# Attention, an ELU MLP and a soft mixture of experts in one kernel: row maxima in one pass of PE, combine weights after the slot inputs, more and longer expert loads

## The chip, the core and the metric

The kernel runs on one core of a Trainium2 chip. The metric is the device time of one execution in microseconds, the median of three runs; the profile is one further execution. TensorE is PE in the profile, VectorE DVE, ScalarE ACT, GpSimd POOL, SyncE SP.

## What is computed

The output of an attention (4 batches, 8 heads, 1152 keys, 576 pooled queries, 64 wide) goes through an ELU MLP and then a soft mixture of experts, all in fp32. Cut to its core:

```python
q_pool = q.reshape(B, H, S // 2, 2, D).mean(axis=3)
scores = scale * np.matmul(q_pool, k.transpose(0, 1, 3, 2))
scores = scores - np.max(scores, axis=-1, keepdims=True)
attn = np.exp(scores); attn = attn / (attn.sum(-1, keepdims=True) + 1e-09)
x = (attn @ v) as [2304 tokens, 512]
h = x @ w_in                                  # [512, 2048]
x = np.where(h > 0, h, np.exp(np.minimum(h, 0)) - 1) @ w_out
logits = x @ phi                              # 8 experts x 4 slots = 32 columns
d = softmax of logits over the tokens; slot_input = d.T @ x
slot_out[e] = np.maximum(slot_input[e] @ w1[e], 0) @ w2[e]   # w1[e] [512, 1024], w2[e] [1024, 512]
c = softmax of logits over the slots; out = c @ slot_out
```

## The kernel before

**Order of the work.** Every operation is handed to a planner (class Plan, line 51) with `add(t, engines, durations, fn, r, w)`: a due time t, the engines that may do it, an estimated duration on each, what it reads and writes. `run` simulates the five queues and sets each engine's instructions in a fixed order; where an operation may go to ACT, DVE or POOL, the cost in `BIAS` of its phase (0 attention, 1 MLP, 2 experts, 3 preparation) is added before the earliest end wins, and `PRI` shifts due times by class. On the chip each engine works through its queue in that order and waits on semaphores. The due times come from constants such as `SLOT`, `OFF`, `TM2`, `EAV`.

**Attention.** 16 pairs of heads. `prep_q` and `prep_k` transpose q and k of a pair and split them into a rounded part and a rest. `max_unit` and the carried part of `step` compute scores for the row maxima alone (line 596), `max_red` reduces them on DVE into MX (line 605). `max_end` (line 633) finishes them: DVE reduces to one column of MZ, PE multiplies MZ by the identity (`row`, line 642) so that the maxima of half the queries (288) lie in a row of a PSUM bank psC, and ACT writes the negated row to nm (line 649). `step` then computes transposed scores, 128 keys by 288 queries by two heads, as four fp32r products, the last of which adds nm (line 664); ACT takes the exponential (676), PE multiplies with v in fp32 into psC (671), and POOL or DVE sums the exponentials (685).

**MLP.** 32 slots: eight groups of 256 hidden columns times four batches (batches 0 to 2 first, then batch 3). In each slot `h_mm` (line 828) multiplies with w_in, `elu` makes the activation on ACT and DVE (839, 840, 842) and splits it into a rounded part (cast, line 500) and a rest (subtraction, line 503), and `o_mm` (line 867) multiplies with w_out into psC, which DVE adds to X (line 878). `split_w` and `split_x` split weights and inputs in the same way; subtractions may go to DVE or POOL. The first stretch also holds `decode` (lines 457 to 497), which prepares the weights: seven DVE steps, of which the addition (line 477) may go to POOL.

**Soft mixture.** `logits` or `logits_split`, then `col_max` (softmax over tokens) and `tok_all` per batch: transposes of X (1030), slot inputs (1034), and in the same function the combine weights: row maximum, exponential (1047), splitting (1001 to 1003), transposes (1053) into C3T.

**Experts.** The expert weights are 64 loads of 512 KB (units), issued by SP (line 1176). `spare` declares the slots of 4 KB per partition that come free as memory of earlier stages dies: 18 of them before the MLP ends, seven in the region z when it has ended; later units reuse slots. `stage1` (1191) multiplies the slot inputs with w1, four experts side by side in 32 columns each; `stage2` (1219) multiplies with w2, first the output columns 0 to 255 (m=0) of all experts into one bank, then columns 256 to 511 (m=1). `finish` (1232, 1250) turns each half into output tiles, scaled by ACT or DVE, and stores them in three pieces.

Of the kernel before, what the change touches and what calls it, by code (L numbers as in the profile page):

```python
# [50 lines left out]
class Plan:  # L51
# [11 lines left out]
    def add(self, t, eng, dur, fn, r=(), w=(), size=0.0, mode="F", port=False, fixed=False):  # L63
# [218 lines left out]
def attention_moe_softmoe(  # L282
# [112 lines left out]
    r0 = zr + 2 * KD * NQ  # L395
# [10 lines left out]
    MZ = carve("f", "MZ", 1, 2 * len(NT5) * D)[0].rearrange("p (a j m) -> p a j m", j=2, m=D)  # L406
# [41 lines left out]
    DN = carve("f", "DN", 1, len(NT5) * NS)[0]  # L448
# [59 lines left out]
    nc.vector.memset(r32(MEM["v"][:, :512]), 1.0)  # L508
    nc.vector.memset(MZ, 0.0)
# [816 lines left out]
```

## Time and profile before

| what | value |
|---|---|
| three runs | 1018.55, 1019.13 (median), 1020.74 us |
| profiled execution | 1019.5 us, its span 1017.7 us |
| PE busy | 979.6 us, 96% |
| DVE, POOL, ACT busy | 690.6, 591.7, 498.4 us |
| HBM read, written | 100.27 MB, 13.18 MB |

The span runs from the first to the last instruction. Busy time is time in which an engine has an instruction in work; a PE that is busy may still be slowed by its operands. The attention stage lasts to some 470 us, the MLP from there to 921, the expert stage to the end. Records of neighbours on one engine can overlap, since an instruction starts before the one ahead of it has fully ended.

### The profile page before, as it was taken

To read this page: it belongs to the slowest core of one execution; us is meant where nothing else is said; L and a number is where in the kernel's file an instruction comes from. 1 tells how busy PE (TensorE), PEld (TensorE's weight loads), DVE (VectorE), ACT (ScalarE), POOL (GpSimd) and SP (SyncE) were. 2 spreads that over 40 slices of the span, in tenths; PEclk is the share of its full clock that TensorE was granted. 3 is DMA by queue.
4 is the path that set the end of the run, shared out by engine and by line. 5 is a ranking of instruction groups with operands and counts; after the bars stand their busy time and mean duration, and the time that the engine had idled before them with its cause. 6 is when DMAs were issued, how large, how long until landed. Compare 5 with 4: busy or idle time off the path is not lost.

```text
span 1017.7 us, 21700 instructions
## 1 busy us (share of the span) xinstructions
PE 979.6 (96%) x8838; PEld 806.5 (79%) x8838; DVE 690.6 (68%) x1141; ACT 498.4 (49%) x886; POOL 591.7 (58%) x389
## 2 busy tenths in 40 slices
PE   7999999999999999999999999999999999998884
PEld 6777777767777777777799999999999999995332
DVE  4776687899888777779888788776446565654000
ACT  1455555656555555556665344444335665533022
POOL 1679889877989889887754544444227345330000
PEclk9899999999999999999999999999999999999856
DMA  7233324234334431212344333535031123124998
GB/s 168 48 84 71 96 68 117 62 106 114 83 84 105 110 80 45 65 36 85 105 142 139 116 103 115 166 119 180 24 104 41 62 85 105 62 84 148 342 348 299
DMA packets 111827, 114.92 MB, mean 113 GB/s; under 512 B 43632, under 2 KB 83056, under 8 KB 111728
## 3 DMA queue, kind: packets, MB, share of 16 engines
q1 hardware_dynamic: 111728, 113.55, 37.7%
q8 instruction: 69, 1.13, 0.5%
q14 instruction: 30, 0.25, 0.1%
HBM read 100.27 MB, written 13.18 MB: 111 GB/s over the span
## 4 chain that ended last, share of the span: by engine, by line
PE 84%; DVE 8%; DMA 3%; ACT 2%; issue 1%; SPq 0%; ACTq 0%; POOL 0%; DVEq 0%; POOLq 0%
PE psA L828 20%; PE psC L867 19%; PE psC L671 13%; PE psA L664 9%; PE psS L664 5%; PE psA L596 3%; DVE memf L605 2%; DMA memf<-in_moe_w_dram 2%; PE psS L596 2%; PE psA L1191 2%; PE psC L695 1%; PE psC L642 1%; PE psC L705 1%; ACT memf L676 1%; DVE memf L544 1%
## 5 line engine op out<-in xcount | busy, mean ns | idle before, releaser
L685 POOL TENSOR_TENSOR memf<-memf 128x576 f32<-128x576 f32 x246 | 369.7, 1504 | 60.8 <-ACT memf L676 37.4
L867 PE MATMUL psC<-memr,memz 128*128 128x288 f32 x1512 | 225.3, 297 | 2.4 <-ACT memf L500 2.3
L867 PEld LDWEIGHTS psC<-memr,memz 128*128 128x128 f32 x1512 | 207.9, 189 | 6.0 <-ACT memf L500 3.4
L605 DVE TENSOR_REDUCE memf<-psA 128x2 f32<-128x384 f32 (+3 forms) x248 | 161.7, 665 | 50.1 <-ACT memf L676 32.9
L671 PE MATMUL psC<-memf 128*64 128x288 f32 x1152 | 171.3, 419 | 0.0
L503 POOL TENSOR_TENSOR memr<-memf,memr 128x576 fp32r<-128x576 f32 x57 | 87.4, 1537 | 139.8 <-ACT memr L500 120.7
L878 DVE TENSOR_TENSOR memf<-psC,memf 128x288 f32<-128x288 f32 x220 | 99.3, 459 | 96.1 <-PE psC L867 94.8
L676 ACT ACTIVATE memf<-psA 128x576 f32<-128x576 f32 x190 | 122.9, 651 | 78.5 <-PE psA L596 61.2
L828 PE MATMUL psA<-memr,memz 128*128 128x288 f32 x768 | 140.7, 296 | 0.0
L828 PEld LDWEIGHTS psA<-memr,memz 128*128 128x128 f32 x768 | 114.9, 188 | 0.2
L671 PEld LDWEIGHTS psC<-memf 128*64 128x64 f32 x1152 | 69.9, 136 | 48.6 <-issue 8.9
L605 DVE TENSOR_REDUCE memf<-psS 128x2 f32<-128x384 f32 (+3 forms) x127 | 84.0, 661 | 27.2 <-ACT memf L676 17.8
L839 ACT ACTIVATE memf<-psA 128x576 f32<-128x576 f32 x64 | 41.7, 651 | 121.5 <-PE psA L828 120.5
L503 POOL TENSOR_TENSOR memz<-memf,memz 128x1024 fp32r<-128x1024 f32 x23 | 56.4, 2452 | 49.9 <-ACT memz L500 49.9
L676 ACT ACTIVATE memf<-psS 128x576 f32<-128x576 f32 x98 | 63.8, 651 | 35.4 <-PE psS L596 30.1
L500 ACT CAST memr<-memf 128x576 fp32r<-128x576 f32 x87 | 57.3, 673 | 45.2 <-DVE memf L842 40.6
L828 PE MATMUL psA<-memr,memv 128*128 128x288 f32 x384 | 78.2, 296 | 0.0
L664 PE MATMUL psA<-memr 64*128 64x288 f32 x744 | 66.3, 300 | 0.6 <-ACT memf L676 0.3
L828 PEld LDWEIGHTS psA<-memr,memv 128*128 128x128 f32 x384 | 61.7, 188 | 0.8 <-issue 0.4
L664 PEld LDWEIGHTS psA<-memr 64*128 64x128 f32 x744 | 54.4, 185 | 8.3 <-issue 4.4
L664 PE MATMUL psA<-memy 64*128 64x288 f32 x582 | 58.2, 305 | 0.0
L842 DVE SCALAR_TENSOR_TENSOR memf<-memf,psA 128x576 f32<-128x576 f32 x64 | 47.8, 746 | 10.7 <-ACT memf L840 10.7
(206 smaller groups left out, 1542.0 us busy)
## 6 DMA issues: line engine op xcount, KB each, us to landing
memf<-in_moe_w_dram SPq DMA_DIRECT2D x38, 512.0 KB
memf<-wscr SPq DMA_DIRECT2D x32, 512.0 KB
memz<-in_q_dram SPq DMA_DIRECT2D x32, 288.0 KB
memz<-in_k_dram SPq DMA_DIRECT2D x32, 288.0 KB
memf<-in_v_dram SPq DMA_DIRECT2D x16, 576.0 KB
memf<-in_moe_w_in_dram SPq DMA_DIRECT2D x32, 256.0 KB
wscr<-memf SPq DMA_DIRECT2D x32, 256.0 KB
memf<-in_moe_w_out_dram SPq DMA_DIRECT2D x16, 512.0 KB
```

Source lines behind the costliest of these rows:

```text
L500: return lambda e: nc.scalar.copy(out_, in_) if e == "ACT" else nc.vector.tensor_copy(out_, in_)
L503: return lambda e: ENG[e].tensor_tensor(out_, a, b, ALU.subtract)
L596: nc.tensor.matmul(tile_[:m, j, lo : lo + n * MW], lhsT=qkb["qh", i][js, o : o + m], rhs=qkb["kh", i][js, g * MW : (g + n) * MW], start=Tr ...
L605: add(t, "DVE", dve(2 * n * MW), lambda: nc.vector.reduce_max(MX[i][:m, a, :, g : g + n], v4(got(psS, tok)[:m, :, lo : lo + n * MW], n), a ...
L664: nc.tensor.matmul(sp[:, j, :NH], lhsT=qkb[w, i][js, cs] if w else ONER[js], rhs=qkb[m, i][js, hs], start=(x == 0), stop=(x == 3))
L671: nc.tensor.matmul(psC[h][j * D : (j + 1) * D, :NH], lhsT=VR[i][:, j, c], rhs=e[:, j], start=(c == 0), stop=(c == NC - 1))
L676: add(t + 0.01, "ACT", act(NQ, True), lambda: nc.scalar.activation(got(EAf, E_), got(psS, S_)[:, :, :NH], AF.Exp, scale=1.0 / 16.0), r=[S_ ...
L685: ENG[e].tensor_tensor(ac, a, got(EAf, E_), ALU.add)
L828: nc.tensor.matmul(ph[:, t, :NH], lhsT=a, rhs=x, start=(i == 0), stop=(i == 3 * KD - 1))
L842: add(t + 1.2, "DVE", dve(NQ), lambda: nc.vector.scalar_tensor_tensor(got(Ef, uk), got(Uf, ek), -1.0, ph(), ALU.add, ALU.max), r=[ek, A], ...
L867: nc.tensor.matmul(po_(), lhsT=a, rhs=x, start=(i == 0), stop=(i == 3 * GF - 1))
L878: add(t0 + 0.8, "DVE", dve(NH), lambda: nc.vector.tensor_tensor(d, po_(), d, ALU.add), r=[ck], w=XK)
```

## The change

Parts, in the order of the program:
- `max_end`: MZ and the identity (IDR) are fp32r, MZ holds 32 columns per head instead of 64, so both heads make one product of 64 output rows: three matmuls instead of six. ACT writes two pieces of 32 rows, and nm is cleared once at the start.
- `max_red` of a carried part is ordered behind the exponential of the same bank.
- The split inputs x of batches 1 and 3 move from region r to region z, which grows by 4.5 slots.
- `tok_all` keeps the slot inputs; the combine weights become `combine(b, t)`, due after the slot inputs of all batches, with a copy of the logits (DN) for each batch.
- Region z gives eleven late slots instead of seven. Units: w1 per expert with whole rows (4 KB runs), w2 of experts 0 to 5 with whole rows (2 KB runs), w2 of the last two experts by halves as before (1 KB runs). `stage2` does both halves of an expert together, but for the last two.
- Output stores are due behind the last load ("loads").
- The planner's numbers are new: `PRI` has 80 entries, `BIAS`, `LOOK`, `SLOT`, `OFF`, `TM2` and others change, and loads of phase 2 count for 0.75 of their size.

```diff
-BIAS = [{'DVE': 2.612, 'Pool': 1.8312, 'ACT': 1.5924}, {'DVE': 3.8592, 'Pool': 2.61, 'ACT': -4.78}, {'DVE': 7.9625, 'Pool': 27.723, 'ACT': 7.0754}, {'ACT': -9.5594, 'Pool': -3.8076, 'DVE': -9.6637}]
+BIAS = [{'DVE': 2.6845, 'Pool': 1.8955, 'ACT': -0.4027}, {'DVE': -3.2955, 'Pool': 5.8552, 'ACT': -4.78}, {'DVE': 7.9625, 'Pool': 25.9664, 'ACT': 7.8882}, {'ACT': -14.3311, 'Pool': 2.7731, 'DVE': -2.1432}]
...
-    MZ = carve("f", "MZ", 1, 2 * len(NT5) * D)[0].rearrange("p (a j m) -> p a j m", j=2, m=D)
+    MZ = carve("v", "MZ", 1, len(NT5) * D)[0].rearrange("p (a j m) -> p a j m", j=2, m=D // 2)
+    IDR = carve("v", "IDR", 1, P)[0]
...
+    for i in range(2):
+        nc.gpsimd.memset(r32(qkb["nm", i]), 0.0)
...
-                for j in range(2):
-                    nc.tensor.matmul(psC[h][j * D : (j + 1) * D, lo - h * NH : hi - h * NH], lhsT=MZ[:, a, j], rhs=ident[:, lo - o : hi - o],
-                                     start=True, stop=True)
+                nc.tensor.matmul(psC[h][:D, lo - h * NH : hi - h * NH], lhsT=MZ[:, a].rearrange("p j m -> p (j m)"), rhs=IDR[:, lo - o : hi - o],
+                                 start=True, stop=True)
...
-        add(t, "PE", 0.476, row, r=[("MZ", 0, a) for a in tiles], w=[("C", h)], mode="C", fixed=True)
-        add(t + 0.01, "ACT", act(NH, True), lambda: nc.scalar.mul(v3(qkb["nm", i], 2)[:, h], psC[h][:, :NH], -1.0), r=[("C", h)], w=[("nm", i, h)])
+        add(t, "PE", 0.15, row, r=[("MZ", 0, a) for a in tiles], w=[("C", h)], mode="C", fixed=True)
+        for j in range(2):
+            add(t + 0.01 + 0.01 * j, "ACT", act(NH, True), lambda j=j: nc.scalar.mul(
+                v3(qkb["nm", i], 2)[j * D : j * D + D // 2, h], psC[h][j * D // 2 : (j + 1) * D // 2, :NH], -1.0), r=[("C", h)], w=[("nm", i, h, j)])
...
+    def combine(b, t):
...
-    spare("z", 0, ts(32.55), 7)
+    spare("z", 0, ts(32.55), 11)
...
-    units = [(1, g, i, c, j) for g in range(NGR) for i in range(2) for c in range(KD) for j in range(2)]
-    units += [(2, e, m, k) for m in range(2) for e in range(NE) for k in range(2)]
+    units = [(1, g, c, y) for g in range(NGR) for c in range(KD) for y in range(NQD)]
+    units += [(2, e, q) for e in range(NE - NLAST) for q in range(4)]
+    units += [(3, e, m, k) for m in range(2) for e in range(NE - NLAST, NE) for k in range(2)]
...
-            src, a = w1[e : e + 2, c * P : (c + 1) * P, i * HF : (i + 1) * HF].rearrange("e p f -> p e f"), 2
+            src, a = w1[NQD * g + y, c * P : (c + 1) * P, :].rearrange("p (i f) -> p i f", i=2), 2
+        elif units[u][0] == 2:
+            _, e, x = units[u]
+            src, a = w2[e, 2 * x * P : 2 * (x + 1) * P, :].rearrange("(x p) f -> p x f", p=P), 2
...
+    for b in range(B):
+        combine(b, t + CMB + 9 * b)
```

**First order view: SP at the end of the program.** Line 1176 before (1214 after) is a unit's load, memzq and memyq are regions z and y in their last use, 506 (514) are other transfers.

Before:

```order
L1176 DMA memf<-in_moe_w_dram 128x2x512 x5
L1176 DMA memzq<-in_moe_w_dram 128x2x512 x7
L1176 DMA memyq<-in_moe_w_dram 128x2x512 x4
L1176 DMA memf<-in_moe_w_dram 128x2x512 x3
L1176 DMA memf<-in_moe_w_dram 128x4x256 x9
L1176 DMA memzq<-in_moe_w_dram 128x4x256 x7
L1176 DMA memyq<-in_moe_w_dram 128x4x256 x4
L1176 DMA memf<-in_moe_w_dram 128x4x256 x12
L506 DMA out_dram<-memf 128x6x256 x6
```

After:

```order
L1214 DMA memf<-in_moe_w_dram 128x1024 x3
L1214 DMA memzq<-in_moe_w_dram 128x1024 x11
L1214 DMA memyq<-in_moe_w_dram 128x1024 x3
L1214 DMA memyq<-in_moe_w_dram 128x2x512
L1214 DMA memf<-in_moe_w_dram 128x2x512 x12
L1214 DMA memzq<-in_moe_w_dram 128x2x512 x11
L1214 DMA memyq<-in_moe_w_dram 128x4x256 x4
L1214 DMA memf<-in_moe_w_dram 128x4x256 x4
L514 DMA out_dram<-memf 128x6x256 x6
```

Behind the 18 early loads stand eleven into region z instead of seven, and their shapes show the runs: 1024, 512 or 256 columns of four bytes.

**Second order view: DVE in the MLP stage, between two ELU steps (842 before, 864 after).** 878 (900) adds an output chunk to X, 480 to 492 (488 to 500) are steps of the decode with the addition 477 (485), 503 (511) is a subtraction.

Before:

```order
L842 SCALAR_TENSOR_TENSOR memf<-memf,psA_79 128x576
L487 TENSOR_SCALAR memf<-memf 128x512
L878 TENSOR_TENSOR memf<-psC_81,memf 128x288
L503 TENSOR_TENSOR memr<-memf,memr 128x576
L878 TENSOR_TENSOR memf<-psC_80,memf 128x288
L489 SCALAR_TENSOR_TENSOR memf<-memf 128x512
L480 TENSOR_SCALAR memf<-memf 128x512
L878 TENSOR_TENSOR memf<-psC_81,memf 128x288
L878 TENSOR_TENSOR memf<-psC_80,memf 128x288
```

After:

```order
L864 SCALAR_TENSOR_TENSOR memf<-memf,psA_79 128x576
L491 TENSOR_SCALAR memf<-memf 128x512
L493 SCALAR_TENSOR_TENSOR memf<-memf 128x512
L900 TENSOR_TENSOR memf<-psC_81,memf 128x288
L495 TENSOR_SCALAR memf<-memf 128x512
L900 TENSOR_TENSOR memf<-psC_80,memf 128x288
L511 TENSOR_TENSOR memr<-memf,memr 128x576
L497 SCALAR_TENSOR_TENSOR memf<-memf 128x512
L485 TENSOR_TENSOR memf<-memf 128x512
L900 TENSOR_TENSOR memf<-psC_81,memf 128x288
L900 TENSOR_TENSOR memf<-psC_80,memf 128x288
```

Over the whole program POOL had 57 subtractions of 576 columns, 30 of 1024 and 24 additions of the decode; it now has no subtraction and 3 additions, and DVE has the others.

**Third order view: PE at the end of the expert stage.** 1219 (1265) is stage 2 into psC_80 (m=0) or psC_81 (m=1), 1232 (1278) begins the finish of a half, 1250 (1296) makes two output tiles.

Before:

```order
L1219 MATMUL psC_80<-memf 32x256 x32
L1219 MATMUL psC_80<-memzq,memf 32x256 x28
L1232 MATMUL psB_6133<-memf 96x256
L1219 MATMUL psC_81<-memyq,memf 32x256 x4
L1250 MATMUL psB_6134<-memr 128x256 x2
L1250 MATMUL psA_78<-memr 128x256 x2
L1250 MATMUL psB_6133<-memr 128x256 x2
L1250 MATMUL psA_79<-memr 128x256 x2
```

After:

```order
L1265 MATMUL psC_80<-memzq,memf 32x256 x4
L1265 MATMUL psC_81<-memzq,memf 32x256 x4
L1265 MATMUL psC_80<-memyq,memf 32x256 x16
L1265 MATMUL psC_81<-memf 32x256 x4
L1278 MATMUL psB_6140<-memf 96x256
L1265 MATMUL psC_81<-memf 32x256 x4
L1296 MATMUL psB_6139<-memr 128x256 x2
L1296 MATMUL psA_78<-memr 128x256 x2
L1296 MATMUL psB_6140<-memr 128x256 x2
L1296 MATMUL psA_79<-memr 128x256 x2
L1265 MATMUL psC_81<-memf 32x256 x8
L1296 MATMUL psB_6139<-memr 128x256 x2
```

Before, 64 matmuls of m=1 (16 loads) follow the start of the first half's finish or stand beside it; now the finish of m=0 starts when all but 12 matmuls of m=1 (three loads) have been issued.

## Rows read from the trace of the kernel before

**Rows 1.** First line of the page: the profiled span.
```profile
span 1017.7 us, 21700 instructions
```

**Rows 2.** Stages: stretch, us, then busy us of PE, PEld, DVE, ACT, POOL.
```profile
200.00:300.00 100.00, 97.87 (x1076) 71.53 (x1074) 87.12 (x133) 57.59 (x99) 85.00 (x57) 1.00 0.37 97
...
505.00:921.00 416.00, 415.11 (x3111) 408.78 (x3109) 282.33 (x512) 200.87 (x352) 182.91 (x106) 1.00 0.32 103
...
600.00:700.00 100.00, 100.00 (x757) 100.00 (x756) 80.68 (x153) 43.45 (x64) 43.83 (x27) 1.00 0.43 134
...
960.00:980.00 20.00, 13.13 (x113) 2.93 (x106) 0.00 (x0) 0.37 (x1) 0.00 (x0) 0.61 1.10 348
```

**Rows 3.** Waits of PE, the longest in total: us, times, longest one.
```profile
PE psC L1219 <- DMA memf<-in_moe_w_dram: 7.7, 12, 0.9
```

**Rows 4.** Timeline of PE in the attention stage: start, us, instructions.
```profile
37.73 0.25 PE L596 MATMUL psS<-memr 64*128 64x192 f32 x2
37.82 0.36 PE L596 MATMUL psA<-memr 64*128 64x384 f32 x2
...
39.76 0.67 PE L642 MATMUL psC<-ident,memf 128*64 128x96 f32 x12
40.35 0.44 PE L596 MATMUL psS<-memr 64*128 64x384 f32 x2
```

**Rows 5.** The instructions of line 642: ns min/median/max, first and last start.
```profile
L642 PE MATMUL psC<-ident,memf x384: 192/272/473, 28.2 to 464.2; 128*64 128x128 f32 x96, 128*64 128x32 f32 x32, 128*64 128x96 f32 x32, 128*64 128x64 f32 x32
```

**Rows 6.** Chain of waits, a piece of the MLP stage: start, us, what.
```profile
510.94 1.59 PE psC L867 x12
```

**Rows 7.** Timeline of PE around one transpose of combine weights.
```profile
866.50 0.27 PE L1053 MATMUL psB<-ident,memr 128*96 128x128 f32 x1
866.61 0.60 PE L1030 MATMUL psB<-ident,memf 128*128 128x128 f32 x4
```

**Rows 8.** Groups by line and shape, 505 to 921 us: busy us, mean ns, idle before.
```profile
L503 POOL TENSOR_TENSOR memr<-memf,memr 128x576 fp32r<-128x576 f32 x53 | 80.9, 1530 | 135.7 <-ACT memr L500 116.6 <-issue 11.5 <-PE psB L1034 6.4
...
L503 POOL TENSOR_TENSOR memz<-memf,memz 128x1024 fp32r<-128x1024 f32 x22 | 53.5, 2432 | 49.9 <-ACT memz L500 49.9
...
L477 POOL TENSOR_TENSOR memf<-memf 128x512 f32<-128x512 f32 x20 | 27.5, 1377 | 24.6 <-DVE memf L489 19.9 <-PE psC L867 2.4 <-PE psA L828 2.3
...
L503 DVE TENSOR_TENSOR memr<-memf,memr 128x576 fp32r<-128x576 f32 x23 | 32.7, 1425 | 5.8 <-ACT memr L500 4.0 <-PE psA L905 1.5
```

**Rows 9.** The subtractions of line 503 on DVE: ns min/median/max.
```profile
L503 DVE TENSOR_TENSOR memr<-memf,memr x31: 741/1576/2273, 195.2 to 905.8; 128x576 fp32r<-128x576 f32 x31
...
L503 DVE TENSOR_TENSOR memz<-memf,memv x1: 1214/1214/1214, 474.3 to 474.3; 128x1024 fp32r<-128x1024 f32 x1
```

**Rows 10.** Timeline of DVE in the MLP stage: start, us.
```profile
640.25 0.74 DVE L842 SCALAR_TENSOR_TENSOR memf<-memf,psA 128x576 f32<-128x576 f32 x1
640.91 0.69 DVE L492 SCALAR_TENSOR_TENSOR memf<-memf 128x512 f32<-128x512 f32 x1
```

**Rows 11.** Timeline of SP: DMA issues of the tail.
```profile
921.11 4.49 SPq L1176 DMA_DIRECT2D memzq<-in_moe_w_dram  x7
...
939.93 1.93 SPq L1176 DMA_DIRECT2D memyq<-in_moe_w_dram  x4
...
994.92 17.19 SPq L506 DMA_DIRECT2D out_dram<-memf  x6
```

**Rows 12.** DMA view, 900 to 1018 us: GB/s in 40 slices of 2.95 us.
```profile
GB/s 5 0 26 157 0 0 0 96 308 387 383 69 0 20 259 322 401 343 360 350 349 348 348 349 348 347 351 344 349 351 348 347 348 348 383 381 74 340 340 114
```

**Rows 13.** Timeline of PE in the expert stage.
```profile
938.83 1.93 PE L1191 MATMUL psA<-memyq,memf 128*32 128x512 f32 x16 [0.24 <-DVE memf L1278]
...
978.24 1.08 PE L1219 MATMUL psC<-memzq,memf 128*32 128x256 f32 x8 [0.51 <-DMA memzq<-in_moe_w_dram]
...
1002.00 1.08 PE L1219 MATMUL psC<-memf 128*32 128x256 f32 x8 [0.30 <-DMA memf<-in_moe_w_dram]
...
1005.66 0.80 PE L1250 MATMUL psB<-memr 96*128 96x256 f32 x2 [0.92 <-DVE memr L1234]
```

More of the change, by code (lines that the diff above doesn't have):

```diff
@@ L447, in attention_moe_softmoe @@
     DT = carve("f", "DT", 1, NQ)[0]
-    DN = carve("f", "DN", 1, len(NT5) * NS)[0]
+    DN = [(lambda i=i: MEM["y"][:, 4 * ND + i * len(NT5) * NS : 4 * ND + (i + 1) * len(NT5) * NS]) for i in range(B - 1)]
+    for i in range(B - 1):
+        plan.region(("DN", i), BASE["y"] + 4 * ND + i * len(NT5) * NS, BASE["y"] + 4 * ND + (i + 1) * len(NT5) * NS)
+    DN += carve("f", "DN", 1, len(NT5) * NS, first=B - 1, late=True)
     M2 = carve("f", "M2", 1, len(NT5))[0]
@@ L600, in v4, with max_red @@
         return ap.rearrange("p j (g k) -> p j g k", g=n)
-    def max_red(tok, p, a, g, n, lo, t):
+    def max_red(tok, p, a, g, n, lo, t, behind=()):
         i = p % 2
@@ L626, in attention_moe_softmoe @@
             own[p] += [(a, g, *MAX2[h][x]) for x, (a, g) in enumerate(cells[h][:nown])]
-            units = [u for u in range(-14, 4)][10 * h : 10 + 8 * h]
-            rest = [(a, g + y) for a, g in cells[h][nown:] for y in range(2)]
+            units = [u for u in range(UC, UC + 18)][10 * h : 10 + 8 * h]
+            rest = sorted(((a, g + y) for a, g in cells[h][nown:] for y in range(2)), key=lambda x: x[1] // 4)
             for u, x in zip(units, rest, strict=True):
@@ L968, in tok_all, with dn @@
         tb, tc_ = ("B", "tb", b), ("C", 0) if last else ("B", "si", b)
-        dn, dr, c3 = v3(DN, n5), v3(DR, n5), v3(C3, n5)
-        DK, RK = [("DN", 0, i) for i in range(n5)], [("RS5", 0, i) for i in range(n5)]
+        dr = v3(DR, n5)
+        DK = [("DN", b, i) for i in range(n5)]
+        def dn():
+            return v3(DN[b](), n5)
         def pc():
@@ L1181, in stage1 @@
     def stage1(u, t):
-        _, g, i, c, j = units[u]
-        if j == 0:
+        _, g, c, last = units[u]
+        if last < NQD - 1:
             return
-        A, pt = ("A", "e", g, i), ("B", "e", g, i)
-        x = i
-        def mm():
-            o = got(psA, A)[:, 0]
-            for y in range(NQD):
-                nc.tensor.matmul(o[y * MQ : (y + 1) * MQ], lhsT=SIZv[:, c, NQD * g + y], rhs=v3(raw(u - 1 + y // 2)[1](), 2)[:, y % 2],
-                                 start=(c == 0), stop=(c == KD - 1))
@@ new lines, in stage2, with mm @@
+    def stage2(u, t):
+        e = units[u][1]
+        whole = units[u][0] == 2
+        if whole and not units[u][2] % 2:
+            return
+        for m in range(2) if whole else [units[u][2]]:
+            k = units[u][2] // 2 if whole else units[u][3]
+            def mm(m=m, k=k):
+                for y in range(NQD):
+                    if whole:
+                        w = v3(raw(u - 1 + y // 2)[1](), 2)[:, y % 2, m * HM : (m + 1) * HM]
+                    else:
+                        w = v3(raw(u)[1](), 4)[:, y]
+                    nc.tensor.matmul(psC[m][y * MQ : (y + 1) * MQ, :HM], lhsT=Gv[:, e // NQD, k, y, e % NQD], rhs=w,
+                                     start=(e == 0 and k == 0), stop=(e == NE - 1 and k == 1))
+            add(t + 0.1 * m, "PE", 0.45, mm, r=[raw(u)[0], ("G", 0, e // NQD, k)] + ([raw(u - 1)[0]] if whole else []), w=[("C", m)], mode="Q")
@@ L1264, in finish @@
                 dma(t + 2.7 + 0.3 * (x + per), out[t0 * P : (x + per) * P, m * HM : (m + 1) * HM].rearrange("(a p) c -> p a c", p=P),
-                    OSB[:, t0 : x + per], [("OSB", 0, y) for y in range(t0, x + per, per)], [("out", m, t0)], 512 * OGRP * HM, 0.5)
-    t = ts(NSLOT) + 8 + 7 + 1.2 * 4 + 4
+                    OSB[:, t0 : x + per], [("OSB", 0, y) for y in range(t0, x + per, per)] + [("loads", 0)], [("out", m, t0)], 512 * OGRP * HM, 0.5)
+    t = ts(NSLOT) + 8 + 7 + TDT[-1] * 4 + 4
     R2 = 2 * NS
```

229 lines of the change are left out of this document (122 added, 107 removed).

## Prediction

> **What bounds the kernel now.** The profiled execution took 1019.5 us: a span of 1017.7 [rows 1] and 1.8 us around it. The median of the three runs is 1019.13, 0.4 us lower; the sum below is made against 1019.5. About 0.2% (2 us) is what a measurement of this kernel can tell from no change.
>
> I read the busy times of whole stages first [rows 2]. In the attention stage (200 to 300 us) PE is busy 97.9 of 100 us, with POOL at 85 and DVE at 87 close behind. In the MLP stage (600 to 700) PE is busy all 100 us, DVE 81. In the expert stage (960 to 980) PE has work for 13 of 20 us, the other engines for almost none, and the DMA moves 348 GB/s. So there are two limits: TensorE up to about 921 us, the transfers behind that. The waits agree: the longest total on PE is that of the second expert matmuls for their weights, 7.7 us [rows 3]. An edit that takes work from PE counts in full before 921; behind it, only what starts a transfer earlier or moves it faster counts.
>
> **Term 1, the rows of maxima.** In the timeline of PE [rows 4] L642 starts at 39.76 and the next instruction at 40.35: 0.59 us for 288 columns, six fp32 matmuls recorded as twelve. There are 32 such pieces (384 records, from 28.2 to 464.2 us [rows 5]); start to next start they sum to 20.5 us, 30 of them at 0.59 to 0.66, one at 0.95, and the first, at a lower clock, at 1.21. After the change a piece is three fp32r matmuls for the same 288 columns. No row shows just that. Lower bound: an fp32r pair of 192 columns starts at 37.73 and its successor at 37.82 [rows 4], 0.09 us, so 288 columns at that pace are 0.14. Upper bound: three whole MLP matmuls, of which twelve take 1.59 us [rows 6], 0.40 in all. I take 0.20, nearer the pair, because these are as narrow as it is; three weight loads keep it above 0.14. The saving is 20.5 - 32 x 0.20 = 14.1 us (7.7 to 16.0). PE then runs 3% faster past POOL and DVE at 85 and 87 of 100, where it already idles 2.1 us per 100 [rows 2]. I give back 2.5 us (0 to 5) for more such waits. The 32 extra ACT instructions cost nothing: ACT is busy 58 of 100 us there, and the row is wanted two steps after it is made; were that slack gone, each would cost some 0.4 us. **Net -11.5 us.**
>
> **Term 2, combine weights.** Fifteen transposes on L1053 lie before 921 us in the order of before, four in that of the change. One starts at 866.50, its successor at 866.61 [rows 7]: 0.11 us. Eleven are 1.2 us, less where they hide: **-1 us** (0 to -1.5). Their ACT and DVE parts lay beside PE. Behind the slot inputs they sit where PE waits for transfers.
>
> **Term 3, the subtractions leave POOL.** The new costs (BIAS) take all of the MLP stage's subtractions and most of the decode's additions from POOL and give them to DVE (second order view). From 505 to 921 us POOL has 53 of 576 columns, 22 of 1024 (seven more read memv) and 20 additions of 512 [rows 8]. On DVE undisturbed the first two take 0.741 and 1.214 us [rows 9], an addition about as much as the 0.69 of L492 [rows 10]: 39 + 35 + 14 = 88 us more. Part comes back: beside POOL the same subtraction on DVE has a median of 1.576 [rows 9], and the 23 with a mean of 1.425 [rows 8] would shrink to 0.741, 16 us. DVE goes from 282 busy us of 416 [rows 2] to about 354, 85%. The dense part is slots 1 to 19, where the decodes lie: per slot eight accumulations of 0.46, two L842 of 0.74, two subtractions of 0.74, 1.3 decodes of about 3.9 and 1.0 for weights: 12.7 us, against 96 PE matmuls at 0.1325, also 12.7. But a recorded duration overlaps its successor: L842 starts at 640.25 with 0.74, the next at 640.91, 0.66 later [rows 10]. With 22 instructions at 0.08 less the need is about 11 of 12.7. So PE stays the bound with little room; in an in-order queue that full, some evictions of psC come late, and PE waits for its bank. I take 0.2 us in each of 19 slots: **+4 us** (0 to +14).
>
> **Term 4, the tail.** Before: seven loads are issued at 921.1, then nothing until stage 1 has freed a slot at 939.9 [rows 11]. The slices of 2.95 us [rows 12] show it: 387 and 383 GB/s, then 69, 0 and 20 over 8.9 us (0.7 us of work), so 8.2 us idle. After: eleven loads (first order view), 5.77 MB, at 385 about 15 us: until 921 + 2 + 15 = 938. Stage 1 starts as late as before, 17.7 us behind the last MLP matmul (921.1 to 938.83 [rows 13]): the logits now come behind two transposes, some 1 us later, but no transposes of weights delay the sum of the slot inputs. It frees its first slots after two groups, about 1.8 us, and data follow 1.7 us later, at 942: a gap of 4 us, **-4.2**. Then 24 loads in 2 KB runs: slices with 2 KB runs show 385, those with 1 KB runs 348 [rows 12], 1.362 against 1.507 us per load, **-3.5**. The 4 KB runs of stage 1 I price as 2 KB ones.
> Against it: the first half of the output is done late. In before its last matmul runs at 978.24 [rows 13], 24 us ahead of that of the last load; in the change only four loads, 6.0 us, follow it (third order view). Its matmul comes 1.7 us after its data, takes 1.1, and 3.66 us lie from there to the first output product (1002.00 to 1005.66 [rows 13], matmul included): the first product 0.3 us after the loads' end, and the first output data some 2.8 later, as in the second half of before (1005.66 to about 1008.5 [rows 12]). So 3.1 us of idle DMA, against the 2.3 of the gap between the halves now (the slice at 74), which mostly stays, as two expert units stand between the products. **+2** (0 to +4). "Outputs last" as such costs nothing: before, the outputs are issued from 994.92, behind the last load, too [rows 11].
> Net -6 (-12 to 0).
>
> A rule that speaks against the 3.5: the Trainium skill, "DMA: Bandwidth & Descriptors", section "Where 436 GB/s comes from", says that HBM to SBUF transfers are bound by about 358 GB/s per core. By it longer runs could gain 24 x 0.04, 1 us, and the sum would be 2.5 us higher. The slices at 387 and 383 GB/s [rows 12] lie above that figure, so I go by the slices.
>
> **Sum.** 1019.5 - 11.5 - 1 + 4 - 6 = 1005. The planner's other numbers move the start-up, the hand-over from attention to the MLP and the decodes; no row prices that. PE's idle time there bounds a gain, a few us in all, a few late transfers a loss: -2 (-6 to +4). **1003 us.**
>
> **Rivals.**
> *DVE becomes the bound of the MLP stage* (the other side). If recorded durations don't overlap and each of 22 instructions waits a further 0.09, a slot needs 12.7 + 2.0, and PE loses 2 us in each of 19 slots: 38 instead of the 4 taken, 1037 us. It decides from about 0.85 us per slot beyond the 0.2, where the 16.5 us forecast are eaten. For it: the dense slots above. Against it: the overlap in rows 10, and that POOL's interference (1.576 against 0.741) goes. 8%.
> *The tail gives nothing*: stage 1 starts 3 us later, and the late first half costs 3 more: 1009. For it: the new order of transposes ahead of the logits. 14%.
> *Long runs move no faster than short ones*: 24 loads stay at 1.507, 1006.5 us. This is what the skill's rule above would do here. Against it stand the slices at 387, but two slices of a burst into idle queues are few. 8%.
> *Everything moves as far as it can*: a row piece at 0.14 and nothing given back (-16), no late evictions (0), tail -9, hand-over -3: 1019.5 - 16 - 1 - 9 - 3 = 990.5. For it: none of the four is against a row. 15%.
> *My forecast*, 1003, within 997 to 1009: 55%.
>
> **Chances.** Faster by over 0.2% (under 1017): the forecast and three rivals, 92%, less 2% for sums of bad ends: 0.90. Within 0.2%: 0.03. Slower: 0.07. The range from 989 to 1014 leaves out the DVE rival and small ends.
>
> **What would show it.** Row pieces on PE at 0.15 to 0.3 us; a pair of heads every 27.4 us, where 15.5 pairs from 28.2 to 464.2 [rows 5] make 28.1 now; in the MLP stage DVE near 85%, PE idle under 6 us, and nothing on POOL; the last MLP matmul near 910 us; eleven loads in a row behind it, a DMA gap of 3 to 5 us instead of 8.2, and slices near 385 GB/s through most of stage 2. Wrong if PE waits for L900 or L511 on DVE in every slot, if a row piece takes 0.4 or more, or if the outputs leave more than 5 us of idle DMA behind the last load.

## The result, and the profile after

The changed kernel takes 1009.63 us (median of four runs, 1006.30 to 1010.63), the kernel before 1019.93 in the runs beside it: ratio 0.9892, 95% interval 0.9863 to 0.9921. It is faster, by 10.3 us where 16.5 were forecast, and inside the range of 989 to 1014; it lies 0.6 us above the 997 to 1009 to which I gave 55%. Its profiled execution took 1009.69 us:

```profile
span 1007.9 us, 21047 instructions
```

The span is 9.8 us shorter than in [rows 1]. It falls into four pieces. The landmarks are two of the 32 rows of maxima, the third (the second pair's first, 54.33 us before, 56.52 after) and the 30th (the fifteenth pair's second, 437.96 and 435.09), and the issue of the first late load (921.11 [rows 11] and 916.13).

| piece | before | after | difference |
|---|---|---|---|
| start-up and first pair | 54.33 | 56.52 | +2.2 |
| thirteen and a half pairs | 383.63 | 378.57 | -5.1 |
| last pair and a half, hand-over, MLP | 483.15 | 481.04 | -2.1 |
| tail | 96.6 | 91.8 | -4.8 |

**One row of maxima on PE**, timeline of the kernel before, then of the changed one (start, us, instructions). L671 and L689 are the product with v, L642 and L658 the row, L596 and L613 the scores for the maxima.

```profile
151.21 1.19 PE L671 MATMUL psC<-memf 128*64 128x288 f32 x8
152.23 0.67 PE L642 MATMUL psC<-ident,memf 128*64 128x96 f32 x12
152.83 0.44 PE L596 MATMUL psA<-memr 64*128 64x384 f32 x2
```

```profile
152.99 1.19 PE L689 MATMUL psC<-memf 128*64 128x288 f32 x8
154.11 0.36 PE L658 MATMUL psC<-memv 128*64 128x96 f32 x3
154.40 0.44 PE L613 MATMUL psS<-memr 64*128 64x384 f32 x2
```

From start to next start the row falls from 0.60 to 0.29 us, but the product ahead of it grows from 1.02 to 1.12. Records of both lines read 1.19; only the starts tell. All 27 rows of the thirteen and a half pairs read so: 0.60 to 0.66 us before (one, with a wait, 0.95), 0.28 to 0.30 after.

**MLP stage** of the changed kernel, the columns of [rows 2]:

```profile
500.00:915.00 415.00, 413.81 (x3103) 407.45 (x3102) 341.92 (x629) 190.63 (x328) 4.43 (x4) 1.00 0.31 106
600.00:700.00 100.00, 100.00 (x755) 100.00 (x754) 89.91 (x170) 43.41 (x63) 0.00 (x0) 1.00 0.33 111
```

DVE is at 82% over the stage and 90% in its dense part, POOL all but empty, PE full. Without work on POOL the subtraction of 576 columns takes 0.751 us on DVE, 1.425 before [rows 8] (groups by line and shape, 505 to 915 us):

```profile
L511 DVE TENSOR_TENSOR memr<-memf,memr 128x576 fp32r<-128x576 f32 x71 | 53.1, 751 | 6.2 <-ACT memr L508 6.0
```

**Tail** of the changed kernel: SP's issues, the DMA rate in 40 slices of 2.7 us from 900 to 1008, and stretches of 5 us with the granted clock of PE (the third number from the right).

```profile
916.13 6.68 SPq L1214 DMA_DIRECT2D memzq<-in_moe_w_dram  x11
938.42 2.18 SPq L1214 DMA_DIRECT2D memyq<-in_moe_w_dram  x4
...
991.73 10.26 SPq L514 DMA_DIRECT2D out_dram<-memf  x6
```

```profile
GB/s 0 194 0 6 0 3 185 411 413 419 413 299 0 0 109 287 328 405 388 385 392 381 388 385 388 385 388 388 374 349 349 347 344 61 227 340 340 339 339 162
```

```profile
920.00:925.00 5.00, 3.38 (x17) 1.61 (x15) 3.27 (x9) 2.75 (x8) 0.00 (x0) 1.00 1.03 415
925.00:930.00 5.00, 4.43 (x18) 2.62 (x19) 2.18 (x11) 2.84 (x14) 0.00 (x0) 0.50 1.03 415
930.00:935.00 5.00, 4.22 (x24) 2.41 (x23) 2.11 (x8) 1.15 (x6) 0.00 (x0) 0.82 0.34 135
935.00:940.00 5.00, 5.00 (x33) 1.36 (x36) 0.00 (x0) 0.39 (x2) 0.00 (x0) 0.66 0.14 29
```

Eleven loads run at 411 to 419 GB/s, stage 2 at 381 to 392 (348 in [rows 12]). The gap is still there: 299, 0, 0 and 109 are 10.8 us with 2.75 us of work at 400 GB/s, so 8 us idle as before. The first reissue leaves 22.3 us behind the first late load, 18.8 before [rows 11]. PE runs at 1.2 GHz (0.50) for 10.2 us of that way (925.0 to 931.8 and 935.2 to 938.6). Its timeline there, the wait ahead of the transposes and the first matmuls of stage 1:

```profile
925.06 0.26 PE L1005 MATMUL psB<-ident,memf 32*64 32x32 f32 x1 [1.68 <-ACT memf L957]
...
934.97 3.46 PE L1229 MATMUL psA<-memyq,memf 128*32 128x512 f32 x16
938.18 5.12 PE L1229 MATMUL psA<-memf 128*32 128x512 f32 x44
```

Of the signs that the prediction named, the row at 0.15 to 0.3 us, the 82% of DVE, the empty POOL and the full PE came, and most of stage 2 near 385 GB/s. A pair of 27.4 us did not: 433.8 us from the first row to the last make 28.0 a pair (28.1 before). Nor did the gap of 3 to 5 us, and the last MLP products end at 915.9, not near 910.

### The profile page after: what moved, and what is told of

The parts are those of the page before. It is cut to its first block, busy times and chain, and to the rows that moved or that the text cites. A ratio compares the mean times of both kernels' runs of the same rounds, so it can differ in the third digit from the quotient of the medians.

```text
span 1007.9 us, 21047 instructions
## 1 busy us (share of the span) xinstructions
PE 968.3 (96%) x8550; PEld 791.4 (79%) x8550; DVE 763.3 (76%) x1281; ACT 497.0 (49%) x887; POOL 396.8 (39%) x278
## 4 chain that ended last, share of the span: by engine, by line
PE 83%; DVE 9%; DMA 5%; issue 1%; ACT 1%; SPq 1%; DVEq 0%; POOL 0%; ACTq 0%; POOLq 0%
PE psC L889 20%; PE psA L850 20%; PE psC L689 13%; PE psA L682 10%; PE psS L682 4%; DMA memf<-in_moe_w_dram 3%; PE psA L613 3%; DVE memf L622 2%; PE psS L613 2%; PE psC L723 1%; PE psC L713 1%; PE psA L597 1%; DMA memzq<-in_moe_w_dram 1%; DVE memf L556 1%; PE psA L574 1%
## 5 line engine op out<-in xcount | busy, mean ns | idle before, releaser
L689 PE MATMUL psC<-memf 128*64 128x288 f32 x1152 | 174.2, 419 | 0.0
L694 ACT ACTIVATE memf<-psA 128x576 f32<-128x576 f32 x207 | 133.5, 652 | 63.7 <-PE psA L613 51.1
L622 DVE TENSOR_REDUCE memf<-psA 128x2 f32<-128x384 f32 (+3 forms) x236 | 143.3, 619 | 27.2 <-PE psA L613 13.0
L622 DVE TENSOR_REDUCE memf<-psS 128x2 f32<-128x384 f32 (+1 forms) x139 | 102.6, 738 | 35.3 <-PE psS L613 18.7
L689 PEld LDWEIGHTS psC<-memf 128*64 128x64 f32 x1152 | 69.8, 136 | 48.5 <-issue 9.2
L850 PE MATMUL psA<-memz 128*128 128x288 f32 x512 | 93.8, 295 | 0.0
L861 ACT ACTIVATE memf<-psA 128x576 f32<-128x576 f32 x64 | 41.8, 654 | 103.1 <-PE psA L850 103.0
L850 PEld LDWEIGHTS psA<-memz 128*128 128x128 f32 x512 | 76.6, 188 | 0.0
L682 PE MATMUL psA<-memr 64*128 64x288 f32 x816 | 72.2, 299 | 2.9 <-DVE memf L622 2.9
L694 ACT ACTIVATE memf<-psS 128x576 f32<-128x576 f32 x81 | 52.8, 652 | 39.3 <-PE psS L613 35.9
L511 DVE TENSOR_TENSOR memr<-memf,memr 128x576 fp32r<-128x576 f32 x80 | 62.8, 791 | 6.5 <-ACT memr L508 6.0
L850 PE MATMUL psA<-memz,memv 128*128 128x288 f32 x256 | 52.0, 296 | 0.0
L682 PEld LDWEIGHTS psA<-memy 64*128 64x128 f32 x630 | 47.8, 188 | 4.9 <-issue 3.6
L508 ACT COPY memf<-psC 128x288 f32<-128x288 f32 (+1 forms) x66 | 26.3, 398 | 49.5 <-PE psC L1265 26.6
```

The costliest lines, as they stand in the source:

```text
L508: return lambda e: nc.scalar.copy(out_, in_) if e == "ACT" else nc.vector.tensor_copy(out_, in_)
L511: return lambda e: ENG[e].tensor_tensor(out_, a, b, ALU.subtract)
L622: add(t, "DVE", dve(2 * n * MW), lambda: nc.vector.reduce_max(MX[i][:m, a, :, g : g + n], v4(got(psS, tok)[:m, :, lo : lo + n * MW], n), a ...
L682: nc.tensor.matmul(sp[:, j, :NH], lhsT=qkb[w, i][js, cs] if w else ONER[js], rhs=qkb[m, i][js, hs], start=(x == 0), stop=(x == 3))
L689: nc.tensor.matmul(psC[h][j * D : (j + 1) * D, :NH], lhsT=VR[i][:, j, c], rhs=e[:, j], start=(c == 0), stop=(c == NC - 1))
L694: add(t + 0.01, "ACT", act(NQ, True), lambda: nc.scalar.activation(got(EAf, E_), got(psS, S_)[:, :, :NH], AF.Exp, scale=1.0 / 16.0), r=[S_ ...
```

## Experiments

In each group one execution is profiled and the others timed; ratios are against the kernel before in the same group. "Thirteen pairs" are counted from the third row of maxima to the 29th: 370.2 us before, 365.4 in the changed kernel.

**1. The row alone in the kernel before**: the part of the diff on MZ, IDR, nm and `row`, planner numbers as before.

```diff
-                for j in range(2):
-                    nc.tensor.matmul(psC[h][j * D : (j + 1) * D, ...
+                nc.tensor.matmul(psC[h][:D, ...
```

> The kernel before with the new row of maxima alone (fp32r, 64 output rows, two ACT pieces, nm cleared at the start), all planner numbers as before. Theory A, from the trace of the changed kernel: the piece on PE falls from 0.61 to 0.29 us, but the product with v ahead of it now ends with a change of type and takes 1.12 instead of 1.02 us, so 0.22 us per piece, 7 us for 32, less about 1 us of new waits for the maxima on DVE and 1 to 2 us of a slower start-up (the clearing of nm on POOL holds up DVE's first small copies): 4 to 6 us faster than before, 1014 to 1016. Rival B, my recorded sum: the piece alone is worth 11.5 us, and what is missing in the changed kernel is lost to its other planner numbers: about 1008.

1020.53 us, ratio 1.0024 (1.0005 to 1.0043): no gain at all, against both theories. The rows take 0.29 us, yet thirteen pairs take 370.3. Busy times from 56 to 437 us, before and in this run (columns of [rows 2]):

```profile
56.00:437.00 381.00, 377.21 (x4162) 277.76 (x4159) 302.26 (x470) 217.38 (x374) 329.73 (x222) 1.00 0.34 88
```

```profile
56.00:437.00 381.00, 371.42 (x3922) 265.66 (x3920) 306.06 (x467) 227.46 (x400) 331.94 (x223) 1.00 0.35 89
```

This run's waits of PE and of DVE (us, times, longest), and the last of them before:

```profile
PE psS L671 <- DVE memf L611: 3.2, 2, 2.1
PE psA L671 <- DVE memf L611: 2.2, 2, 1.5
...
DVE memf L611 <- ACT memf L683: 43.2, 66, 1.6
```

```profile
DVE memf L605 <- ACT memf L676: 43.3, 69, 1.6
```

What PE saved, 5.8 us, it now stands idle (9.6 us instead of 3.8), 5.4 of it in waits for reductions of the maxima on DVE (here L611). These for their part wait 43 us for exponentials on ACT (L683), as they did before; with a faster PE that wait reaches it.

**2. The same products in fp32 in the changed kernel.**

```diff
- lhsT=MZ[:, a].rearrange("p j m -> p (j m)"), rhs=IDR[:, lo - o : hi - o],
+ lhsT=r32(MZ[:, a]).rearrange("p j m -> p (j m)"), rhs=ident[:, lo - o : hi - o],
```

> The changed kernel with the same three products per row of maxima in fp32 instead of fp32r, in the same order; nothing else differs. Theory A: the piece goes back to 0.5 to 0.6 us and the product with v ahead of it back to 1.02, so 0.2 us per piece and 6 to 7 us in all, less the waits for DVE that this hides: 3 to 7 us slower than the changed kernel (1013 to 1017). Rival C, that another engine (POOL or DVE) sets the pace of a pair in the changed kernel: under 2 us slower (1009 to 1011.5), pairs of heads still 28.0 us.

1013.07 us, ratio 0.9937 (0.9920 to 0.9954), 3.4 us slower than the changed kernel by the medians, 4.6 by the ratios; thirteen pairs 370.8, 5.5 more. Theory A holds. Timeline of PE:

```profile
154.61 1.19 PE L689 MATMUL psC<-memf 128*64 128x288 f32 x8
155.63 0.66 PE L658 MATMUL psC<-ident,memv 128*64 128x96 f32 x6
156.22 0.44 PE L613 MATMUL psS<-memr 64*128 64x384 f32 x2
```

The product is back at 1.02, the row at 0.59: the type alone decides, 0.20 us per row net, and in this order PE sets the pace. Three fp32 products take as long as the six before (0.60), so making them fewer was worth nothing by itself.

**3. The row issued twice.**

```diff
-            for a in tiles:
+            for a in tiles + tiles:
```

> The changed kernel with the three fp32r products of each row of maxima issued twice. If the 0.29 us of a piece are mostly changes of type and shape at its ends (0.10 us each), the second set costs 0.12 to 0.17 us: pieces of 0.42 to 0.46, and with PE as the only bound 4 to 5 us slower than the changed kernel. If each of these narrow products costs 0.1 us by itself, pieces of 0.57 to 0.6 and 9 us slower. If another engine sets the pace of a pair, under 2 us slower whatever the piece.

1014.07 us, ratio 0.9944 (0.9925 to 0.9962), 4 to 5 us slower. Timeline of PE:

```profile
152.58 1.19 PE L689 MATMUL psC<-memf 128*64 128x288 f32 x8
153.71 0.54 PE L658 MATMUL psC<-memv 128*64 128x96 f32 x6
154.17 0.44 PE L613 MATMUL psS<-memr 64*128 64x384 f32 x2
```

Six products take 0.46 (median 0.47), three 0.29: a set costs 0.18 by itself. The other 0.11 of a piece I put down to the change at its end, from products of 128 rows and 64 columns (128\*64) to the packed ones of 64 rows (64\*128); no run takes that change away alone.

**4. Subtractions back on POOL.**

```diff
-{'DVE': -3.2955, 'Pool': 5.8552, 'ACT': -4.78}
+{'DVE': 3.8592, 'Pool': 2.61, 'ACT': -4.78}
```

> The changed kernel with the old costs of the MLP stage (BIAS[1]): the planner puts 69 subtractions and most additions of the decode on POOL again; the order of the attention stage is unchanged. My recorded step says that moving them to DVE costs 4 us: then this is 4 us faster than the changed kernel (about 1005.5). Theory A, from the changed kernel's trace (PE busy 99.5 to 100 of 100 us in the MLP stage): the step costs nothing, so 0 to 1 us either way. Rival D: POOL beside DVE slows both (1.43 instead of 0.74 us for a subtraction on DVE), and the move gained what PE waited for before: 1 to 4 us slower.

1009.50 us, ratio 0.9899 (0.9883 to 0.9916): no difference. DVE is busy 78 of 100 us (90 in the changed kernel) and PE 100 in both; from the last row of maxima to the first late load 453.8 us against 453.0. Theory A. Its profile reads 1.00, 1.00, 0.86, 0.80 where the changed kernel's clock reads 1.00, 0.50, 0.82, 0.66, and its first reissue comes 19.9 us behind the first late load instead of 22.3: the hint for run 7.

**5. The attention stage's old planner numbers** in the changed kernel (PRI entries of phases 0 and P out, too).

```diff
-BIAS = [{'DVE': 2.6845, 'Pool': 1.8955, 'ACT': -0.4027}, ... {'ACT': -14.3311, 'Pool': 2.7731, 'DVE': -2.1432}]
+BIAS = [{'DVE': 2.612, 'Pool': 1.8312, 'ACT': 1.5924}, ... {'ACT': -9.5594, 'Pool': -3.8076, 'DVE': -9.6637}]
```

> The changed kernel with the planner's numbers of the attention stage as before (no PRI entries of phases 0 and P, the old BIAS[0] and BIAS[3]); rows of maxima in fp32r, MLP and tail as changed. Theory E, after the row alone brought nothing in the old order (28.0 to 29.9 us per pair, PE idle 9.6 us of 381, mostly waiting for maxima on DVE): the cheaper row is worth its 5 to 6 us only in the new order, which puts 7 accumulations from POOL onto DVE and the reductions in another place; here 13 pairs take 369 to 371 us as in the kernel before (365.4 in the changed kernel), and the run is 4 to 6 us slower than the changed kernel (1013.5 to 1016). Rival F, that the wait in that run came from one late decode step on DVE (4.3 us at 160.9): 13 pairs in 365 to 367 us, within 2 us of the changed kernel.

1010.70 us, ratio 0.9897 (0.9874 to 0.9921); thirteen pairs 365.8. Theory E falls: these numbers are worth nothing that can be measured, as rival F had it. What does carry the gain is seen in runs 8 and 9.

**6. Seven late slots, and, apart from it, short runs.**

```diff
-    spare("z", 0, ts(32.55), 11)
+    spare("z", 0, ts(32.55), 7)
```

> The changed kernel with seven late slots in region z instead of eleven. If transfers alone bound the tail, the four loads that no longer fit ahead of stage 1 move behind the gap in the DMA: 4 x 1.27 us (512 KB at 412 GB/s) = 5 us slower than the changed kernel, about 1014.5, the gap about 13 us instead of 8. Rival G: what ends the gap is the first freed slot, and stage 1 on PE needs no more than seven loads by then, so that part of it is made good behind: 0 to 3 us slower.

1012.22 us, ratio 0.9915 (0.9896 to 0.9935), 2.6 slower by the medians. In the profile the gap is 11.5 us (slices 173, 0, 0, 0, 123) instead of 8, and from the first late load to the end 97.5 us instead of 91.8. The medians make the four loads worth 2.6 us (2.3 by the ratios), the tails of the two profiles 5.7; with the intervals overlapping, this doesn't tell rival G from the 5.

```diff
-NLAST = 2
+NLAST = 8
```

> The changed kernel with all of w2 loaded by halves in 1 KB runs (NLAST = 8) as before the change; eleven slots and 4 KB runs of w1 stay. By my recorded terms 24 loads take 1.507 instead of 1.362 us, 3.5 us, and the first half of the output is ready in time again, -2: 1.5 us slower, about 1011. Theory H, from the changed kernel's trace (386 GB/s in stage 2, outputs 2.1 us behind the last load, 1.5 before): the late half costs under 1 us, so 3 us slower, about 1012.5. Rival I, long runs no faster than short ones: 0 to 2 us faster than the changed kernel.

1009.92 us, ratio 0.9893 (0.9873 to 0.9913): no difference by the medians. But its profile shows less of the low clock, 20.6 us to the first reissue; behind that it takes 72.2 us, the changed kernel 69.5. Unclear, so it was repeated as run 11.

**7. Useless products where PE waits**: 12 ahead of the transposes L1005, 4 behind them, 8 ahead of L1321. Their operand is the split phi, and nothing reads their result.

```diff
+                psC[1][:NS, :256], lhsT=f[:, :NS], rhs=f, start=True, stop=True), r=r + [("PH", 0)], w=[("WU", 0), ("C", 1)])
...
+            fill(12, tq + 0.8, [("LT", 0, b, h) for h in range(2)])
+            fill(4, tq + 1.0, [tb])
+            fill(8, tq + 1.0 + 4 * dt + 2.5, [tc_])
```

> The changed kernel with 24 small products of no use (32 x 256, 0.107 us each) put where PE waits between the last logits and stage 1; their result is never read. In the changed kernel's profile the granted clock of PE is at half from 925.0 to 931.8 and from 935.2 to 938.6 us, and the first reissued load comes 22.3 us behind the first late load; in the run with the subtractions on POOL only 933.6 to 937.0 is at half, and it is 19.9 us. Theory J: the low clock costs 2 to 2.4 us there, and if PE has work its clock stays up: 19 to 20 us to the first reissue, 1.5 to 2.5 us faster than the changed kernel (about 1007.5). Rival K: the clock falls all the same, or the extra products delay the chain: 0 to 1.5 us slower.

1004.66 us, ratio 0.9837 (0.9820 to 0.9855): faster than both kernels. Stretches as above, SP, and the DMA slices of 2.7 us from 900 on:

```profile
925.00:930.00 5.00, 4.55 (x28) 3.20 (x27) 1.69 (x7) 2.23 (x13) 0.00 (x0) 1.00 0.97 394
930.00:935.00 5.00, 4.85 (x45) 1.58 (x49) 0.78 (x3) 0.36 (x2) 0.00 (x0) 1.00 0.38 108
```

```profile
913.87 7.90 SPq L1224 DMA_DIRECT2D memzq<-in_moe_w_dram  x11
932.33 1.76 SPq L1224 DMA_DIRECT2D memyq<-in_moe_w_dram  x4
```

```profile
GB/s 46 149 0 6 3 123 382 375 407 419 398 42 185 395 379 398 388 386 387 388 387 386 385 387 387 384 356 347 350 348 193 2 291 214 336 340 339 226 0 0
```

The clock stays at 2.4 GHz, the reissue comes 18.5 us behind the first late load, and the gap shrinks to 3.9 us (42 and 185 in 5.4 us). The tail takes 89.1 us instead of 91.8. That is 2.7 of the 5 us. The rest stands ahead of the late loads in these two profiles, in the start-up, where the two kernels are alike: the third row starts at 54.05 us instead of 56.52. That the medians' other 2.3 us are the spread between executions is not shown. The reissue comes 18.5 us behind the first late load in all three runs with the products (7, 10 and 11), and 19.9 to 22.3 behind it in the seven other profiles of kernels with eleven late slots.

**8. Without the order behind the exponential**, in the changed kernel.

```diff
-            max_red(S_, *more, 1, NH, t + 0.02, [("SX", p, u)])
+            max_red(S_, *more, 1, NH, t + 0.02)
```

> The changed kernel without the one new order in max_red: the reduction of a carried part of the maxima is no longer ordered behind the exponential of the same bank; everything else as changed. Theory L: on the chip the reduction waits for that exponential in any case (DVE waits 43 us of 381 for L676 before, 43 us in the run with the row alone, 22 us where the order is told to the planner), and a planner that doesn't know it lets DVE stand at the head of its queue; with the faster PE that delay reaches PE. Then DVE's waits for the exponential go back to about 40 us, 13 pairs take 369 to 371 us instead of 365.4, and the run is 4 to 6 us slower than the changed kernel (1013.5 to 1015.5). Rival M, the other new numbers carry it: 365 to 367 us, within 2 us of the changed kernel.

1017.04 us, ratio 0.9963 (0.9952 to 0.9975), 7.4 us slower. Thirteen pairs take 369.0, PE is idle 7.6 us of 381, and from the first to the last row of maxima it takes 441.1 us, 433.8 with the order. Waits of DVE in this run, then in the changed kernel:

```profile
DVE memf L622 <- ACT memf L694: 47.3, 69, 2.0
DVE memf L622 <- PE psA L613: 6.0, 18, 0.6
DVE memf L622 <- PE psS L613: 4.4, 12, 0.9
```

```profile
DVE memf L622 <- ACT memf L694: 21.6, 53, 1.4
DVE memf L622 <- PE psS L613: 17.0, 39, 1.0
DVE memf L622 <- PE psA L613: 12.1, 23, 0.7
```

In the thirteen pairs theory L holds: 3.7 us more, and DVE's waits for the exponential are back. Its waits for scores on PE go the other way, 10 us here and 29 with the order, so the order moves DVE's waiting more than it shortens it (58 us to 51 in all three lines). What goes beyond it lies in the last pair, where the 31st and the 32nd row are 18.1 us apart instead of 12.9: PE waits there for an exponential and for a sum on POOL, and its granted clock is 0.50 for 3.4 us behind that (466.9 to 470.3).

```profile
461.85 0.80 PE L682 MATMUL psA<-memr 64*128 64x288 f32 x8 [2.22 <-ACT memf L694]
...
465.65 0.71 PE L713 MATMUL psC<-memf 128*64 128x288 f32 x4 [1.79 <-POOL memf L703]
```

```profile
465.00:470.00 5.00, 4.35 (x28) 2.42 (x28) 3.98 (x5) 2.82 (x5) 2.20 (x3) 0.69 0.74 255
```

**9. The row and that order in the kernel before**: run 1 and

```diff
-            max_red(S_, *more, 1, NH, t + 0.02)
+            max_red(S_, *more, 1, NH, t + 0.02, [("SX", p, u)])
```

> The kernel before with the new row of maxima and with the reduction of a carried part ordered behind the exponential of the same bank: two parts of the change, the planner's numbers as before. Theory L: DVE's waits for the exponential fall from 43 to about 22 us, PE's idle time in 381 us from 9.6 to about 4, 13 pairs take 365 to 366 us instead of 370.3, and the run is 4 to 6 us faster than with the row alone (1014 to 1016.5). Rival M: 369 to 371 us, no faster than with the row alone (1020.5).

1022.82 us, ratio 1.0014 (1.0000 to 1.0029). Half of theory L is there: DVE waits 20.9 us for the exponential, PE is idle 4.2 us, thirteen pairs take 367.6 instead of 370.3. As a time nothing comes of it, as from the last row of maxima to the first late load 461.1 us pass (457.3 before, 453.0 in the changed kernel). Part of that can be placed: PE's first products of the MLP wait 2.4 us for an exponential (L683), and from 511.4 us the granted clock is 0.50 for 3.4 us (0.98 in the mean of 505 to 600, 1.00 before). Why the old numbers lose there with this order stays open.

```profile
PE psA L835 <- ACT memf L683: 2.4, 1, 2.4
```

**10. Useless products, and nm cleared behind the ones on POOL.**

```diff
-        nc.gpsimd.memset(r32(qkb["nm", i]), 0.0)
...
+        add(-90 + i, "Pool", 0.6, lambda i=i: nc.gpsimd.memset(r32(qkb["nm", i]), 0.0), w=[("nm", i, h, j) for h in range(2) for j in range(2)])
```

> The run with 24 useless products ahead of stage 1 (1004.7 us), and nm cleared on POOL behind the ones instead of at the very start. In the changed kernel DVE's first two small copies take 1.3 us beside the clearing (0.3 and 0.2 before) and the warm-up of PE begins at 3.06 instead of 2.28 us. If the start-up hangs on that, the first row of maxima starts 0.8 us earlier and the run is 0.5 to 1 us faster: 1003.7 to 1004.2. Rival N: the first loads and PE's clock set the start-up (the first row starts between 28.4 and 32.3 us in runs with the same start), and nothing changes: 1004 to 1005.5.

1004.82 us, ratio 0.9840 (0.9826 to 0.9854): nothing. The warm-up begins at 2.01 us and the first row of maxima at 29.21 all the same. Rival N.

**11. Useless products, and all of w2 in 1 KB runs** (the edit of run 7 with `NLAST = 8`).

> The run with 24 useless products ahead of stage 1 (1004.7 us), with all of w2 in 1 KB runs by halves (NLAST = 8). Without the products the halves made no difference that the medians could show (1009.9 against 1009.6), but there the low clock ahead of stage 1 differed in the two profiles, and behind the first reissued load the halves took 2.7 us longer (72.2 against 69.5). With the clock settled, theory H gives 2 to 3.5 us slower than the run with the products: 1006.7 to 1008. By my recorded terms (3.5 for the runs less 2 for the late half) 1.5 slower: 1006. Rival I, nothing or a gain: 1003 to 1005.

1006.92 us, ratio 0.9857 (0.9841 to 0.9873), 2.1 to 2.3 us slower than runs 7 and 10 by the medians, 1.7 to 2.0 by the ratios; its tail takes 89.8 us against 89.1 and 88.8. The sign is that of the long runs, the size 1 us by the profiles and 2 by the medians: my recorded 1.5 lies between.

## Why the prediction was right or wrong

**The bound** was read rightly: PE to the end of the MLP (100 of 100 us there after too), transfers behind it. 10.3 us came of 16.5, and one term explains most of the difference. That the sum is off by no more is partly luck: a loss that I charged for the subtractions did not come and made good for a part of what that term lacks.

**Term 1 was mis-sized: 11.5 us in the sum, 9.7 of them for 27 of the 32 rows, where 5.1 were measured.** Two errors of about equal size, and one omission.
- *The row's own time.* I took 0.20. The products cost 0.18 (run 3), but the piece takes 0.29, as something, probably the change of tile shape, is added at its end: 32 x 0.09 = 2.9 us.
- *The neighbour.* The 0.59 of [rows 4] ended with the change from fp32 to fp32r. I counted it as saved; it moved into the product with v, 1.02 to 1.12 (run 2 takes it back): 32 x 0.10 = 3.2 us. The trace of before had the price in it: a product with v ahead of the sums (L695, also fp32 and 128\*64) takes 1.02 from start to start in 28 of 30 cases, ahead of the scores, which differ in type and shape, 1.12 (41.99 to 43.11 below). Both changes together cost no more there than the type alone does here. A row had one change at its end, and the new one has one at either end. So a row saves 0.61 - 0.29 - 0.10 = 0.22 by the medians, in 27 rows 5.9.

```profile
41.99 1.19 PE L671 MATMUL psC<-memf 128*64 128x288 f32 x8
43.11 0.44 PE L596 MATMUL psS<-memr 64*128 64x384 f32 x2
```

- *What I gave back, 2.5 us.* In the changed kernel it is 5.9 - 5.1 = 0.8. But POOL and DVE "close behind" do eat all of a cheaper row if the order stays (run 1). What rescues the gain is one line of the diff that I listed and priced at nothing: told that a reduction waits for the exponential of its bank, the planner puts the reductions at another place in DVE's queue, and DVE waits 22 us for it instead of 47, and more for scores (run 8: worth 3.7 us in thirteen pairs and 5.1 in the last one; run 9 shows that alone it doesn't carry the gain to the end).

By the Trainium skill, "TensorEngine Tiling (Array Packing)", section "Key Properties", changing the tiling mode drains TensorE. The 0.11 us left at the end of the row agree with that; the 0.10 us between fp32 and fp32r products come without any change of shape.

**Start-up: +2.2 us, not forecast.** The second pair's first row starts between 54.0 and 56.9 us in nine profiles of kernels with the changed start (mean 55.6), at 54.3 in the one of before. The traces show what goes with it, the granted clock from 20 to 45 us: 0.80 before and in the three that start by 54.7, 0.73 in the changed kernel and the others between 55.7 and 56.5, 0.66 in the one at 56.9. So the 2.2 us go with a longer stretch at 1.2 GHz. Whether the changed start makes that likelier, one profile of the kernel before can't tell; the clearing of nm has no part that can be seen (run 10). The changed kernel, then run 7:

```profile
20.00:45.00 25.00, 21.33 (x147) 13.95 (x145) 20.93 (x28) 8.46 (x15) 9.27 (x7) 0.73 0.41 93
```

```profile
20.00:45.00 25.00, 22.18 (x173) 14.78 (x175) 21.82 (x29) 9.57 (x17) 11.66 (x8) 0.80 0.37 83
```

**Terms 2 and 3 and the hand-over: +1 in the sum, -2.1 measured.** By their cost in [rows 7] the eleven transposes are 1.2 us, and three more rows of maxima lie in this piece (0.7 us); together that is nearly all of it, so the 2 us that I took off for the planner's other numbers have nothing to show for them. The subtractions cost nothing instead of 4 (run 4): DVE came to 82%, near the 85 forecast, with PE still full. Records that overlap, my argument against the rival, were reason enough not to charge 0.2 us per slot. The rival in which DVE becomes the bound fell.

**Term 4: -6 in the sum, -4.8 measured, with one part wrong.** The 2 KB runs came out as costed, 381 to 392 GB/s, and the 4 KB runs, at 411 to 419, faster than I priced them. The Trainium skill's figure of about 358 GB/s for a core ("DMA: Bandwidth & Descriptors", section "Where 436 GB/s comes from"), which spoke against this, lies below both, so the measurement decides. (By that figure the runs would have gained 1 us; my rival without any gain, at 1006.5, went further than it.) The outputs start 2.1 us behind the last load, 3.1 forecast. But the gap didn't shrink: -4.2 in the sum, 0 measured. I took stage 1 to start as late after the MLP as before, and its first slots to be free 1.8 us later. With eleven loads ending sooner and PE at 1.2 GHz on its way there (stage 1 starts 19.0 us behind the last MLP products, 17.8 before and 16.7 in run 7; its first sixteen matmuls last from 934.97 to 938.18, 3.2 us, where they took 1.75 before) the data came some 8 us behind the loads' end. I read the granted clock of one stage and not that of the hand-over. With the clock held (run 7) the gap is 3.9 us, the 4 that I had put down. The rival "the tail gives nothing" had this mechanism, a late stage 1, but the faster transfers outweighed it.

## What to carry to other kernels

Cost a short matmul by starts, with its neighbours' ends, not by its own records: a change of type or tile shape moves with it. A cheaper instruction on a bounding engine paid here only where the engines close behind it were ordered to follow, so price the ordering edits of a diff too. Look at the granted clock just ahead of a hand-over, where PE waits for small steps of others; a few products of no use can be worth their time there.

## What the runs showed that I had not expected

- Between fp32 and fp32r products of the same shape PE loses 0.10 us (1.12 against 1.02, runs 2 and 3), between 128\*64 and 64\*128 of one type probably 0.11; a change of both at once costs 0.10.
- Behind a wait of PE of 1.68 us (923.4 to 925.06) the granted clock fell to 0.50; with 24 products of 0.1 us in that wait and the next ones (run 7) it stayed at 1.00, and the ten slot-input products (L1041, run 7's L1051) took 2.5 us from start to next start (924.40 to 926.91) instead of 4.5 (927.00 to 931.51).
- 4 KB runs moved 411 to 419 GB/s on one core, 2 KB runs 381 to 392, 1 KB runs 348 [rows 12].
